# A GEGLU feed-forward kernel: first weight loads reordered over two DMA queues, chunk loads on ScalarE's queue, two of four w_down sums moved

## Chip, cores and metric

One core of a Trainium2 chip. The metric is the device time of one execution in microseconds (us). The kernel before had a median of 542.76 us in the three runs (542.32 to 544.04) from which the prediction was made.

## The reference

```python
B, S, D, F = 1, 2048, 1024, 3584            # bf16, all inputs
def reference(x, w_gate, w_up, w_down):
    return (gelu_tanh(x @ w_gate) * (x @ w_up)) @ w_down
```

## The kernel before

The kernel multiplies with a seven-product scheme (Strassen's). Sums and differences of blocks of x and of the weights are formed on VectorE, GpSimd and ScalarE, and TensorE then does seven block products where a plain product needs eight. It adds them up in banks, accumulators of 128 x 512 values; hT is the hidden activation, stored transposed. Work goes in two halves of 1024 tokens. In a half, 14 pairs of 128-wide column blocks (pairs 0 to 13) give hT, and two groups of down products follow. The first half has plain matmuls in place of pairs 0 and 1, the "first units".

Its first lines issue the loads. `sp` and `act` put an instruction on SyncE's or ScalarE's stream in program order, and a DMA issued there goes to that engine's queue (ScalarE's queue: q10 in the page, 0.79 MB).

```python
load_x0(0, sp)                              # x block, 256 columns
load_w(first, 0, 0, 2, act, 0, FA)          # w_gate rows 0 to 2 (of 8 blocks)
load_w(first, 1, 0, 2, sp, 0, FA)           # w_up rows 0 to 2
load_x0(1, act)
for j in range(2):
    load_xT(xT, 0, 0, KH + j, KH + j + 1)   # DMA transpose, SyncE's queue
    load_w(first, j, 2, 5, act, 0, FA)      # rows 2 to 5, gate then up
act(nc.scalar.preload_act_table(ACT.Gelu_apprx_tanh))
# ... 8 matmuls on constants ...
for j in range(2):
    load_w(first, j, 5, KD, sp, 0, FA)      # rows 5 to 8
for kd in range(KH + 2, KD):
    load_xT(xT, 0, 0, kd, kd + 1)
```

Blocks 0 to 3 of x are transposed on TensorE and copied to xT, blocks 4 to 7 come by DMA transpose. A pair then runs as follows, with hooks (`done`) at which other work is inserted:

```python
# one pair, as it runs from the second on
m1 (2 x 4 bf16 matmuls); ScalarE copies the banks
m2 of the pair before (2 x 4): gelu on ScalarE, hT multiply on VectorE
done("m2 of last")
m6, m6; done("m6"); m5, m5   # m5 overwrites the banks that m2's gelu and multiply read
add m5 to the banks on VectorE; done("m5")
m7, m7; done("m7"); s4 products; done("m3"); a22 products; done("m4")
```

At the hooks of the first half the kernel prepares the down products (`steps`: four w_down sums a pair on VectorE, written to a 4-deep ring of buffers; two of every three are stored to DRAM) and the x of the second half (`stage_x`: DMA transpose into the same ring; `store_x`: store to DRAM):

```python
def load_chunk(key=key):                    # every second pair, 2 x 1 MB
    new_chunk(key)
    for j in range(2):
        load_w(key, j, 0, KD)               # SyncE's queue
...
then["m2 of last"] = [lambda q=q: stage_x(*q) for q in xs[:2]] + then.get("m2 of last", [])
then["m7"] = [store_x]
then["m3"] = steps[:1] + [lambda i=i: stage_load(i) for i in new]
then["m4"] = steps[1:]                      # three sums ahead of the next m2 multiply
```

## Time and profile before

| | kernel before |
|---|---|
| median of the first three runs | 542.76 us |
| span of the profiled execution | 540.9 us |
| TensorE busy | 534.2 us, 99% |
| first pair (pair 2) starts | 34.19 us |
| a pair | 12.56 us; pair 9: 13.16 us |
| x stores, issue to landing | median 5.0 us |

TensorE is the bound (99% busy, 95% of the chain that ended last), so the table is about its stream: when the first pair starts tells what the start cost, and the distance from the first bf16 matmul of one pair to that of the next tells what a pair cost. The lines are in the prediction. A busy sum will not do here: this trace misses 36 matmul records (it has 2356), and busy times of pipelined matmuls overlap (a matmul of L252 has 379 ns in the page's mean, and the next starts 0.216 us after it). In the lines, PE is TensorE and PEld its weight loads, DVE is VectorE, ACT ScalarE, POOL GpSimd; SPq and ACTq are what SyncE and ScalarE issue. A bracket gives how long the engine was idle before, and what ended the wait.

### The profile page before, as it was taken

Reading aid. Unit: us, or ns where it says so; the run is one execution under the profiler, and the core shown is the slowest. Engines: PE = TensorE matmul, PEld = TensorE weight load, DVE = VectorE, ACT = ScalarE, POOL = GpSimd, SP = SyncE. Lnnn points to the kernel's source line nnn. Section 1 sums busy time; section 2 is a strip of 40 time slices with the busy share of each in tenths; the row PEclk is TensorE's granted clock in tenths of the full one; section 3 lists DMA queues with packets and bytes.
Section 4 is the critical chain, followed back from the end, with each engine's and each line's share of the span. In section 5 each row is a group of like instructions: output and inputs, shape, how many; then the busy total and the mean of one; then the engine's idle time right before and its main releaser. Section 6 shows DMA issues by size and latency. Waiting matters only on the chain.

```text
span 540.9 us, 7082 instructions
## 1 busy us (share of the span) xinstructions
PE 534.2 (99%) x2356; PEld 374.8 (69%) x2392; DVE 360.4 (67%) x465; ACT 258.4 (48%) x439; POOL 246.0 (45%) x206
## 2 busy tenths in 40 slices
PE   8999999999999999999999999999999999999997
PEld 3457777766676676767776667777777766866865
DVE  0747878787886998889573433444445469969961
ACT  2435555555555319216465555555554552452270
POOL 0187888888887000000046777667777730000000
PEclk9999999999999999999999999999999999999999
DMA  9926495685837976779950405041331456677846
GB/s 221 307 80 209 125 341 161 211 256 191 277 132 227 333 240 219 266 248 311 331 196 1 155 2 155 4 153 42 114 98 59 155 204 209 228 242 247 288 148 205
DMA packets 84771, 102.70 MB, mean 190 GB/s; under 512 B 18688, under 2 KB 66304, under 8 KB 84736
## 3 DMA queue, kind: packets, MB, share of 16 engines
q1 hardware_dynamic: 83136, 101.47, 58.8%
q10 hardware_dynamic: 1600, 0.79, 0.6%
q8 instruction: 19, 0.31, 0.2%
q14 instruction: 16, 0.13, 0.1%
HBM read 85.98 MB, written 12.58 MB: 182 GB/s over the span
## 4 chain that ended last, share of the span: by engine, by line
PE 95%; DMA 3%; issue 1%; POOL 0%; ACTq 0%; DVE 0%; ACT 0%; SPq 0%
PE bank L388 58%; PE bank L658 32%; PE bank L252 5%; DMA x_dram<-o_sb 2%; DMA w_mem<-in_w_up_dram 1%; POOL s_mem L360 0%; ACTq L161 0%; DVE hT L276 0%; ACT o_sb L711 0%; ACTq L167 0%; SPq L161 0%; DVE o_sb L593 0%; ACTq L711 0%; SPq L612 0%
## 5 line engine op out<-in xcount | busy, mean ns | idle before, releaser
L388 PE MATMUL bank<-t_mem,s_mem 128*128 128x512 f32 x1016 | 240.4, 395 | 0.1
L388 PEld LDWEIGHTS bank<-t_mem,s_mem 128*128 128x128 f32 x1016 | 190.8, 188 | 42.5 <-DVE hT L276 0.5
L360 POOL TENSOR_TENSOR s_mem<-w_mem 128x512 fp32r<-128x512 bf16 x100 | 119.3, 1213 | 191.6 <-DVE t_mem L244 102.2
L658 PE MATMUL bank<-t_mem,s_mem 128*128 128x512 f32 x544 | 127.4, 393 | 0.0
L276 DVE TENSOR_TENSOR hT<-w_mem,bank 128x512 bf16<-128x512 f32 x104 | 70.6, 686 | 75.7 <-PE bank L388 42.5
L658 PEld LDWEIGHTS bank<-t_mem,s_mem 128*128 128x128 f32 x544 | 102.0, 188 | 22.5 <-issue 0.5
L411 DVE TENSOR_TENSOR bank<-bank,m 128x512 f32<-128x512 f32 x104 | 68.0, 694 | 56.2 <-ACT m L433 51.9
L388 PE MATMUL bank<-xT,w_mem 128*128 128x512 bf16 x391 | 93.0, 380 | 1.3
L271 ACT ACTIVATE w_mem<-bank 128x512 f32<-128x512 f32 x104 | 61.0, 596 | 62.3 <-DVE bank L411 39.0
L388 PEld LDWEIGHTS <-w_mem 128*128 128x128 bf16 x416 | 38.7, 98 | 49.8 <-issue 6.3
L360 POOL TENSOR_TENSOR s_mem<-w_mem,s_mem 128x512 fp32r<-128x512 bf16 x50 | 65.8, 1337 | 0.0
L568 DVE TENSOR_TENSOR t_mem<-w_mem 128x1024 fp32r<-128x1024 bf16 x56 | 65.6, 1218 | 0.0
L360 POOL TENSOR_TENSOR s_mem<-s_mem,w_mem 128x512 fp32r<-128x512 f32 x50 | 63.2, 1284 | 0.0
L438 ACT COPY bank<-bank 128x512 f32<-128x512 f32 x52 | 29.6, 570 | 38.2 <-PE bank L388 37.9
L373 ACT CAST s_mem<-w_mem 128x512 fp32r<-128x512 bf16 x52 | 32.0, 615 | 29.1 <-PE bank L388 25.4
L633 DVE TENSOR_TENSOR s_mem<-hT 128x512 fp32r<-128x512 bf16 x52 | 35.7, 714 | 10.2 <-PE bank L658 9.4
L658 PEld LDWEIGHTS <-hT 128*128 128x128 bf16 x224 | 21.3, 98 | 26.6 <-issue 2.1
L433 ACT COPY m<-bank 128x512 f32<-128x512 f32 x52 | 30.5, 587 | 17.4 <-PE bank L388 17.4
L442 ACT COPY bank<-bank 128x512 f32<-128x512 f32 x52 | 29.6, 570 | 13.8 <-PE bank L388 13.8
L711 ACT CAST o_sb<-bank 128x512 bf16<-128x512 f32 x28 | 15.3, 585 | 39.7 <-PE bank L658 39.7
L593 DVE TENSOR_TENSOR o_sb<-wd_sb,o_sb 128x512 fp32r<-128x512 bf16 x28 | 33.6, 1200 | 0.4
L252 PE MATMUL bank<-xT,w_mem 128*128 128x512 bf16 x125 | 28.0, 379 | 0.6 <-DMA w_mem<-in_w_up_dram 0.4
(42 smaller groups left out, 252.4 us busy)
## 6 DMA issues: line engine op xcount, KB each, us to landing
t_mem<-t_dram SPq DMA_DIRECT2D x56, 512.0 KB, 5.3
w_mem<-in_w_gate_dram SPq DMA_DIRECT2D x11, 1024.0 KB, 5.5
w_mem<-in_w_up_dram SPq DMA_DIRECT2D x11, 1024.0 KB, 7.9
wd_sb<-in_w_down_dram SPq DMA_DIRECT2D x28, 256.0 KB, 4.4
t_dram<-o_sb SPq DMA_DIRECT2D x28, 256.0 KB, 2.4
wd_sb<-in_w_down_dram SPq DMA_DIRECT2D x12, 512.0 KB, 8.3
w_mem<-in_w_down_dram SPq DMA_DIRECT2D x10, 512.0 KB, 6.2
w_mem<-in_w_down_dram SPq DMA_DIRECT2D x4, 1024.0 KB, 6.6
```

What stands on the lines that cost most here:

```text
L252: nc.tensor.matmul(ps[:], lhsT=w_sb[:, kd, fi * P : (fi + 1) * P], rhs=xT[tb][:, kd, :], start=(kd == 0), stop=(kd == KD - 1),)
L271: act(nc.scalar.activation(out=g_sb, in_=ps[:], func=ACT.Gelu_apprx_tanh))
L276: nc.vector.tensor_tensor(out=hT[:, fc, tb * TB : (tb + 1) * TB], in0=g_sb, in1=ps[:], op=ALU.mult,)
L360: pool(nc.gpsimd.tensor_tensor(out=t, in0=in0, in1=in1, op=op))
L373: act(nc.scalar.copy(out=t, in_=a(1, 1)))
L388: nc.tensor.matmul(banks[bank][:], lhsT=lhs[:, c, :], rhs=rhs[:, c, :], start=start and c == 0, stop=c == KH - 1, skip_group_check=True,)
L411: nc.vector.tensor_tensor(out=banks[dst][:], in0=banks[src][:], in1=m5[j][:], op=ALU.add)
L433: act(nc.scalar.copy(out=m5[j][:], in_=banks[V_[j]][:]))
L568: dve(nc.vector.tensor_tensor(out=t, in0=in0, in1=in1, op=ALU.subtract))
L593: dve(nc.vector.tensor_tensor(out=t, in0=in0, in1=in1, op=ALU.subtract))
L633: dve(nc.vector.tensor_tensor(out=t, in0=in0, in1=in1, op=op))
L658: nc.tensor.matmul(banks[bset[u]][:], lhsT=lhs(i, u), rhs=rhs(i), start=start and i == 0, stop=stop and i == NS - 1, skip_group_check=True,)
```

## The change

Its intent is to have the weights that TensorE needs first in front of the DMA transposes (the first two took SyncE 1.21 and 1.25 us to issue in the trace of before and landed 5.4 and 5.8 us after issue; the loads around them took 0.45 to 0.74 to issue), and to keep VectorE's w_down sums and the 2 MB chunk loads out of each other's way.

```diff
-    for j in range(2):
-        load_xT(xT, 0, 0, KH + j, KH + j + 1)
-        load_w(first, j, 2, 5, act, 0, FA)
+    load_w(first, 0, 2, 5, act, 0, FA)
+    load_w(first, 1, 2, 5, sp, 0, FA)
@@
-    for j in range(2):
-        load_w(first, j, 5, KD, sp, 0, FA)
-    for kd in range(KH + 2, KD):
+    for kd in range(KH, KD):
         load_xT(xT, 0, 0, kd, kd + 1)
+        if kd == KH + 1:
+            for j in range(2):
+                load_w(first, j, 5, KD, act, 0, FA)
@@ transpose_x0: copies of blocks 0 and 1
-            if n % 2 == 0:
+            if q == 0 or n == 0:
                 dve(nc.vector.tensor_copy(...))
@@ first_units: block by block, gate and up in turn
-        order = [(0, 0), (0, 1), (1, 0), (1, 1)]
-        order += [(j, kd) for kd in range(2, KD) for j in range(2)]
-        for j, kd in order:
+        for kd, j in [(kd, j) for kd in range(KD) for j in range(2)]:
@@ load_chunk
-                        load_w(key, j, 0, KD)
+                        load_w(key, j, 0, KD, act)
@@ hooks of the first half
-                then["m2 of last"] = [
-                    lambda q=q: stage_x(*q) for q in xs[:2]
-                ] + then.get("m2 of last", [])
-                then["m7"] = [store_x]
-                then["m3"] = steps[:1] + [lambda i=i: stage_load(i) for i in new]
-                then["m4"] = steps[1:]
+                then["m2 of last"] = (
+                    then.get("m2 of last", [])
+                    + steps[:2]
+                    + [lambda q=q: stage_x(*q) for q in xs[:2]]
+                )
+                then["m7"] = [store_x] + [lambda i=i: stage_load(i) for i in new]
+                then["m4"] = steps[2:]
@@ the hT differences of pairs 7 to 10 (cut: the w_down rows of pair 12 are appended, not set)
-                then.setdefault("m5", []).append(
+                then.setdefault("m6", []).append(
```

More of the change, by code (lines that the diff above doesn't have):

```diff
@@ L847 @@
                 new = range((n[1] + 2) // 3, (n[2] + 2) // 3)
-                then["m2 of last"] = [
-                    lambda q=q: stage_x(*q) for q in xs[:2]
-                ] + then.get("m2 of last", [])
-                then["m7"] = [store_x]
-                then["m3"] = steps[:1] + [lambda i=i: stage_load(i) for i in new]
-                then["m4"] = steps[1:]
+                then["m2 of last"] = (
[5 more added lines that the diff above has]
+                then["m4"] = steps[2:]
                 xs = xs[2:]
             if pair == NPAIR - 2:
-                then["m2 of last"] = [
-                    lambda: load_wd_rows(0, 4),
-                    lambda: load_wd_rows(4, 8),
-                ]
+                then.setdefault("m2 of last", []).extend(
+                    [lambda: load_wd_rows(0, 4), lambda: load_wd_rows(4, 8)]
+                )
             if 6 < pair < 11:
                 i = 2 * pair - 8
-                then.setdefault("m5", []).append(
+                then.setdefault("m6", []).append(
                     lambda i=i: s_down(hT, 0, "s3", i, i + 2)
```

## The prediction

> **What bounds the kernel now.** I read the page's first and fourth parts, then TensorE's own waits, then TensorE's timeline to see where its stream of matmuls breaks.
>
> ```profile
> PE 534.2 (99%) x2356; PEld 374.8 (69%) x2392; DVE 360.4 (67%) x465; ACT 258.4 (48%) x439; POOL 246.0 (45%) x206
> PE 95%; DMA 3%; issue 1%; POOL 0%; ACTq 0%; DVE 0%; ACT 0%; SPq 0%
> ```
>
> TensorE is busy for 534.2 of 540.9 us and is 95% of the chain that ended last. No other engine is above 67%. Waits elsewhere are therefore worth only what they take out of TensorE's stream. The timeline of TensorE matmuls (start, duration, line, count):
>
> ```profile
> 4.48 0.98 PE L302 MATMUL bank<-ident,w_mem 128*128 128x128 bf16 x8
> 5.54 1.46 PE L252 MATMUL bank<-xT,w_mem 128*128 128x512 bf16 x6
> 6.84 0.61 PE L302 MATMUL bank<-ident,w_mem 128*128 128x128 bf16 x8
> 7.28 1.05 PE L252 MATMUL bank<-xT,w_mem 128*128 128x512 bf16 x4
> 8.71 25.64 PE L252 MATMUL bank<-xT,w_mem 128*128 128x512 bf16 x115 [0.38 <-DMA w_mem<-in_w_up_dram]
> ...
> 107.80 3.63 PE L388 MATMUL bank<-xT,w_mem 128*128 128x512 bf16 x15
> 111.08 9.44 PE L388 MATMUL bank<-t_mem,s_mem 128*128 128x512 f32 x40
> 120.36 3.63 PE L388 MATMUL bank<-xT,w_mem 128*128 128x512 bf16 x15
> 123.64 10.04 PE L388 MATMUL bank<-t_mem,s_mem 128*128 128x512 f32 x40
> 133.52 3.63 PE L388 MATMUL bank<-xT,w_mem 128*128 128x512 bf16 x15
> ```
>
> I use start to start, because busy times of pipelined matmuls overlap. In the chain in order of time, 49 matmuls of the first units take 10.74 us plus a step of 0.05: about 0.216 us each. A pair of the main loop is 56 matmuls in 12.56 us (107.80 to 120.36); less 16 bf16 matmuls at 0.216 (3.46) that leaves 9.10 for 40 fp32r matmuls, 0.228 each. Two breaks show:
>
> - **At the start.** Four matmuls from 7.28 need 0.86 us, so the next could start at 8.14; it starts at 8.71, behind the w_up rows 2 to 5. Loss 0.57 us.
> - **In the pair from 120.36**, pair 9. It takes 13.16 us where its neighbours take 12.56. Loss 0.60 us.
>
> All other pairs of the first half keep 12.56 (within 0.01), as do those of the second. At 40 fp32r and 16 bf16 matmuls a pair the kernel from 8.71 on is otherwise one stream; the down products show two more slips of some 0.13 us. The change can therefore win little more than 1.2 us, 0.2%.
>
> The second break is explained by the VectorE and DMA issue lines around it:
>
> ```profile
> 116.11 0.46 SPq L161 DMA_DIRECT2D w_mem<-in_w_gate_dram  x1
> 116.73 0.46 SPq L161 DMA_DIRECT2D w_mem<-in_w_up_dram  x1
> 117.29 1.99 SPq L612 DMA_DIRECT2D x_dram<-o_sb  x2
> ...
> 125.44 0.69 DVE L593 TENSOR_TENSOR o_sb<-wd_sb 128x512 fp32r<-128x512 bf16 x1 [1.37 <-DMA x_dram<-o_sb]
> 126.05 0.68 DVE L276 TENSOR_TENSOR hT<-w_mem,bank 128x512 bf16<-128x512 f32 x1
> 126.78 1.23 PEld L388 LDWEIGHTS bank<-t_mem,s_mem 128*128 128x128 f32 x6 [0.48 <-DVE hT L276]
> ```
>
> The chunk loads (two of 1 MB) enter SyncE's queue ahead of the two stores of x. A store lands 7.6 us after issue in this stretch (median 5.0 over the kernel). A wd sum on VectorE needs the store's buffer, waits 1.37 us, and holds the hT multiply behind it; that multiply must read its bank before product m5 may overwrite it. In the pair before, three wd sums also stand ahead of that multiply, which then ends at 113.68, about 0.1 us before m5's second half starts: the place has no slack.
>
> [...] ScalarE's queue moved 0.79 MB beside SyncE's from the start, at some 320 GB/s together from 3 to 5 us. [...] one wd sum takes 0.69 us at 99.69, where GpSimd is idle, and two take 3.11 us from 109.98 beside GpSimd sums.
>
> **The change part by part.**
>
> *First weights.* Until now the w_up rows 2 to 5 were the fourth load on ScalarE's queue, issued at 2.38 and landing 6.3 us later (8.68), while SyncE's queue sent slow transposes. After, they are third on SyncE's queue (issue near 1.8). Ahead of any transpose stand 576 KB on each queue: 1.18 MB. Up to 5.0 us the old trace moved 0.84 MB (0.03, 0.17 and 0.64 in the stretches 1 to 2, 2 to 3, 3 to 5); the other 0.34 MB at 320 GB/s takes 1.06. I estimate both weight pieces landed by 6.3 to 6.8.
>
> TensorE then does: transposes from 4.48 and first matmul at 5.54 as before (the copies moved from ScalarE to VectorE end at about the same 5.49); four matmuls of block 0 to 6.40; eight transposes, 0.44, to 6.84; four matmuls of block 1 to 7.70; block 2 at 7.70 without a wait. Before, the same work was reached with ten matmuls done and 8.71. Gain: up to 0.57 us.
>
> What could take it back: rows 5 to 8 are now on ScalarE. The built program makes the w_up piece wait for the w_gate rows 2 to 5[...]. So it is issued near 6.6 to 7.1, where it was 4.96. With only 192 KB ahead of it on its queue and half of the 215 GB/s seen from 5 to 9 us, I estimate a landing at 10.1; it is needed at 7.70 + 14 matmuls of 0.216 = 10.72. The margin is 0.6. The transposes of blocks 4 to 7 are needed at 9.43, 10.29, 11.15 and 12.02 and I estimate them 0.7 to 2 us earlier. The next w_gate half (512 KB) is needed at 12.88; before, it landed 4.7 after issue, at 13.05, and it is now issued about 0.9 earlier: 12.1. All margins are positive but below 1 us, so I credit 0.4 of 0.57.
>
> *Chunk loads on ScalarE.* Ten pairs get two issues of about 0.5 us each on ScalarE. They wait for the m2 matmuls, behind which ScalarE has nothing to do: it is idle 1.24 us before its next copy (112.44). That copy may slip by 0.2 us; its reader, m7, comes almost 2 us later. Cost 0. The x stores lose the 2 MB ahead of them, and no longer take 8 us.
>
> *Two wd sums moved up, x transposes behind them.* The same four sums a pair, but two now stand behind the m2 multiply, not ahead of it, in a stretch where GpSimd is idle (until 114.25). The multiply should end near 112.3 instead of 113.68 against m5's 113.8, so a late store no longer reaches TensorE. The buffers of the x stores are next asked for in the following pair, some 7 us after issue instead of about 4. Gain: the 0.60 of pair 9.
>
> The price: two sums (about 2.0) and, in pairs 7 to 10, an hT difference (0.75) come before the m5 additions. From 112.3 that gives 115.05 and the first addition done at 115.75; TensorE needs its bank at 116.6. Margin 0.85, cost 0.
>
> *Sum:* 0.4 + 0.6 = 1.0 us; 542.76 - 1.0 = 541.7.
>
> **The rivals.**
>
> *The late w_up rows 5 to 8 become the new wait.* For: the semaphore wait ties their issue to a landing. Against: no transposes ahead of them on their queue. A landing at 12 would stall TensorE 1.3 us, and the total would be about 542.4.
>
> *ScalarE is blocked by its DMA issues.* The fourth xT copy stands behind that same issue, so it ends near 8.2 (needed at 8.56); and in the loop a chunk load waiting for an old transfer would hold up every copy. Some tenths in each of ten pairs would be 1 to 3 us more: 543 to 545. Against: the semaphores that the chunk loads wait for belong to transfers issued half a pair or more earlier.
>
> *VectorE's additions come late.* If the moved sums take 1.3 each beside GpSimd, and wait for a load, the first addition misses 116.6 in some of eleven pairs: 0.3 each, about 542.5 to 544. Against: the idle of 1.14 before that addition now.
>
> *All of it is hidden.* Then 542.7. Against: both breaks are gaps in TensorE's own stream, which is the end.
>
> **Range and chances.** All three old runs lie between 542.32 and 544.04, so noise is as big as the effect. I predict 541.7, range 540.9 to 543.0. For 2% faster, 10.9 us would have to go, and TensorE has only 6.7 us of idle in all. For 2% slower a new stall of nearly 1 us in each of ten pairs would be needed.
>
> **What would show it.** Right: TensorE's stream of first-unit matmuls unbroken from about 7.3, the first pair starting near 33.7 (34.19 before); pair 9 lasting 12.56; no wait of a wd sum on an x store; x stores landing in 5 us or less beside chunk loads. Wrong: a TensorE wait near 10.7 on w_up or near 12.9 on w_gate; pairs longer than 12.56, above all the even ones; an m5 addition named as TensorE's releaser.

What the text said of the hardware without a trace or run of this case is cut from it, and the places are marked. The sum: 0.4 for the start and 0.6 for pair 9 make 1.0 us, and 542.76 - 1.0 = 541.7. Of the waits on semaphores the two traces show this much: each of the first eight DMAs to use a semaphore a second time waits on it, and the issue of the w_up rows 5 to 8 is one of these (issued at 7.50, its semaphore's last step at 7.48).

## The result, and the profile after

Ratios here are the mean time of one kernel's fast runs over that of the other's of the same rounds, so not quite the ratio of the medians quoted.

The changed kernel had a median of 541.46 us (541.23 to 543.14, six runs) against 543.1 (542.32 to 544.08, six runs): ratio 0.9973, 95% interval 0.9956 to 0.9991. That is the same within 2%, and clear of 1. It was run twice more: 0.9981 (0.9969 to 0.9993) and 0.9984 (0.9973 to 0.9996). So it is 0.2 to 0.3% faster, about 0.9 to 1.5 us.

The first and fourth parts of its page, for the two lines shown of before:

```profile
PE 535.1 (99%) x2392; PEld 374.5 (69%) x2392; DVE 354.9 (66%) x466; ACT 258.9 (48%) x438; POOL 235.0 (44%) x206
PE 98%; DMA 1%; ACTq 0%; ACT 0%; issue 0%
```

The chain is now 98% TensorE, and DMA is down from 3% to 1%. Busy TensorE time rose from 534.2 to 535.1 because no matmul record is missing here, not because it does more. TensorE's timeline (start, duration, line, count):

```profile
4.38 0.62 PE L302 MATMUL bank<-ident,w_mem 128*128 128x128 bf16 x8 [0.18 <-DMA w_mem<-in_x_dram]
5.24 1.02 PE L252 MATMUL bank<-xT,w_mem 128*128 128x512 bf16 x4 [0.24 <-DVE xT L310]
6.10 0.61 PE L302 MATMUL bank<-ident,w_mem 128*128 128x128 bf16 x8
6.55 27.41 PE L252 MATMUL bank<-xT,w_mem 128*128 128x512 bf16 x124
...
119.98 3.63 PE L386 MATMUL bank<-xT,w_mem 128*128 128x512 bf16 x16
123.25 9.44 PE L386 MATMUL bank<-t_mem,s_mem 128*128 128x512 f32 x40
132.54 3.63 PE L386 MATMUL bank<-xT,w_mem 128*128 128x512 bf16 x16
```

The first pair starts at 33.80 (34.19 before), and pair 9 takes 132.54 - 119.98 = 12.56 (13.16 before). The two account for 0.99 of the 1.2 us between the spans (540.9 and 539.7); two slips of 0.12 and 0.14 in the down products of before, absent here, cover the rest.

The start is less clean than one line of 124 matmuls looks. The timeline of the instructions of several engines:

```profile
7.50 0.44 ACTq L161 DMA_DIRECT2D w_mem<-in_w_up_dram  x1
7.52 0.76 PEld L252 LDWEIGHTS <-w_mem 128*128 128x128 bf16 x5 [0.44 <-DMA w_mem<-in_w_gate_dram]
7.98 0.58 ACT L312 COPY xT<-bank 128x512 bf16<-128x512 bf16 x1 [4.31 <-DMA w_mem<-in_w_gate_dram]
...
10.90 11.12 PEld L252 LDWEIGHTS <-w_mem 128*128 128x128 bf16 x53 [0.47 <-DMA w_mem<-in_w_up_dram]
```

The w_gate rows 2 to 5 land at 7.5. Only then can ScalarE issue the w_up rows 5 to 8, whose semaphore they share, and only behind that issue make its copy of xT block 3. The starts of single matmuls in the trace show three gaps, beyond the spacing of 0.216: 0.11 at 7.53, 0.21 at 8.61 and 0.14 at 10.91, together 0.46 us.

Around pair 9 (SyncE's issues and VectorE, for the lines shown of before):

```profile
113.68 2.83 SPq L605 DMA_TRANSPOSE o_sb<-in_x_dram  x2
121.35 0.80 SPq L610 DMA_DIRECT2D x_dram<-o_sb  x2
...
123.31 0.69 DVE L591 TENSOR_TENSOR o_sb<-wd_sb 128x512 fp32r<-128x512 bf16 x1 [0.96 <-DMA x_dram<-o_sb]
123.92 0.68 DVE L276 TENSOR_TENSOR hT<-w_mem,bank 128x512 bf16<-128x512 f32 x1
```

A sum still waits 0.96 us for a store: this was predicted to vanish. But the multiply ends at 124.60, and m5's second half, which needs it, is due about 126.0 (twelve matmuls of 0.228 after 123.25). That leaves 1.4 us, and TensorE does not notice. The median landing of the eight stores and eight transposes of staged x, from the issue lists of before and then of after, tells what was traded:

```profile
x_dram<-o_sb SPq DMA_DIRECT2D x8, 128.0 KB, 5.0
...
o_sb<-in_x_dram SPq DMA_TRANSPOSE x8, 2.8
```

```profile
x_dram<-o_sb SPq DMA_DIRECT2D x8, 128.0 KB, 2.3
...
o_sb<-in_x_dram SPq DMA_TRANSPOSE x8, 4.7
```

By these medians the stores land 2.7 us sooner after issue, but their transposes land 1.9 us later. In the changed kernel it is the four transposes issued beside chunk loads that take 6.3 to 7.6 us; the other four take 2.7 to 3.2.

### The profile page after: what moved, and what is told of

It is laid out like the page before. It is cut to its first block, busy times and chain, and to the rows that moved or that the text cites. A ratio compares the mean times of both kernels' runs of the same rounds, so it can differ in the third digit from the quotient of the medians.

```text
span 539.7 us, 7102 instructions
## 1 busy us (share of the span) xinstructions
PE 535.1 (99%) x2392; PEld 374.5 (69%) x2392; DVE 354.9 (66%) x466; ACT 258.9 (48%) x438; POOL 235.0 (44%) x206
## 4 chain that ended last, share of the span: by engine, by line
PE 98%; DMA 1%; ACTq 0%; ACT 0%; issue 0%
PE bank L386 61%; PE bank L656 33%; PE bank L252 5%; DMA w_mem<-in_w_gate_dram 1%; ACTq L161 0%; ACT xT L312 0%; ACT o_sb L709 0%; ACTq L167 0%; ACTq L709 0%
## 5 line engine op out<-in xcount | busy, mean ns | idle before, releaser
L358 POOL TENSOR_TENSOR s_mem<-w_mem 128x512 fp32r<-128x512 bf16 x100 | 115.8, 1178 | 201.3 <-DMA w_mem<-in_w_up_dram 104.6
L386 PE MATMUL bank<-xT,w_mem 128*128 128x512 bf16 x416 | 94.3, 380 | 0.0
L358 POOL TENSOR_TENSOR s_mem<-w_mem,s_mem 128x512 fp32r<-128x512 bf16 x50 | 62.1, 1267 | 0.0
L358 POOL TENSOR_TENSOR s_mem<-s_mem,w_mem 128x512 fp32r<-128x512 f32 x50 | 59.6, 1212 | 0.0
L631 DVE TENSOR_TENSOR s_mem<-hT 128x512 fp32r<-128x512 bf16 x52 | 34.2, 685 | 10.2 <-PE bank L656 9.5
L591 DVE TENSOR_TENSOR o_sb<-wd_sb,o_sb 128x512 fp32r<-128x512 bf16 x28 | 29.4, 1051 | 0.5
L252 PE MATMUL bank<-xT,w_mem 128*128 128x512 bf16 x128 | 28.4, 379 | 0.3 <-DVE xT L310 0.2
```

The costliest lines, as they stand in the source:

```text
L252: nc.tensor.matmul(ps[:], lhsT=w_sb[:, kd, fi * P : (fi + 1) * P], rhs=xT[tb][:, kd, :], start=(kd == 0), stop=(kd == KD - 1),)
L358: pool(nc.gpsimd.tensor_tensor(out=t, in0=in0, in1=in1, op=op))
L386: nc.tensor.matmul(banks[bank][:], lhsT=lhs[:, c, :], rhs=rhs[:, c, :], start=start and c == 0, stop=c == KH - 1, skip_group_check=True,)
L631: dve(nc.vector.tensor_tensor(out=t, in0=in0, in1=in1, op=op))
```

## The experiments

Twelve kernels ran, all correct. "First pair" and "pair 9" are read from TensorE's timeline as above. "Down wait" is what a down group (43.95 us, to the next group's or half's start) lost when TensorE waited there for saved sums.

| run | edit | first pair at | pair 9 | down wait | median us | ratio (95%) |
|---|---|---|---|---|---|---|
| before | | 34.19 | 13.16 | no | 542.76 | |
| changed | | 33.80 | 12.56 | no | 541.46 | 0.9973 (0.9956 to 0.9991) |
| e0_after_again | changed | 33.87 | 12.56 | no | 541.45 | 0.9981 (0.9969 to 0.9993) |
| h1_after_third | changed | 34.04 | 13.01 | no | 541.47 | 0.9984 (0.9973 to 0.9996) |
| e1_start_only | start of the change | 33.59 | 13.20 | 1.0 | 542.82 | 0.9997 (0.9983 to 1.0011) |
| e2_loop_only | loop of the change | 33.76 | 12.56 | no | 542.65 | 0.9993 (0.9979 to 1.0008) |
| e3_chunks_act_only | chunk loads to ScalarE | 34.21 | 12.56 | 0.95 | 541.95 | 0.9981 (0.9968 to 0.9994) |
| e4_sums_only | loop, chunks on SyncE | 34.07 | 12.56 | no | 541.77 | 0.9977 (0.9965 to 0.9989) |
| e5_copies_only | one copy to VectorE | 33.55 | 13.25 | 0.66 | 541.97 | 0.9993 (0.9981 to 1.0005) |
| e6_copy_kd3_dve | changed + copy | 33.89 | 12.56 | no | 541.53 | 0.9982 (0.9970 to 0.9994) |
| e7_wup_on_sp | changed + w_up on SyncE | 33.55 | 12.56 | 0.86 | 542.08 | 0.9995 (0.9982 to 1.0007) |
| g1_sums_place | sums' place only | 34.72 | 13.48 | no | 543.88 | 1.0024 (1.0012 to 1.0036) |
| g2_chunks_first | queue order only | 34.54 | 12.56 | 0.76 | 541.86 | 0.9995 (0.9975 to 1.0015) |
| f1_b21_on_act | changed + two loads | 33.87 | 12.56 | no | 542.18 | 0.9995 (0.9983 to 1.0007) |

The ratios are to the kernel before in the same rounds: medians 542.92 for e1 to e4, 542.29 for e0 and e5 to e7, 542.51 for g1, g2, f1, h1.

### The two parts alone

e1 has the diff's hunks up to the first units, e2 those behind them.

> The kernel before with the start of the change alone (order of the first weights, three copies on VectorE, block order). My theory, read from the two traces: the changed kernel's first pair starts at 33.80 us instead of 34.19, and pair 9 takes 12.56 instead of 13.16, and these are separate. So here: first pair starts at 33.8 +- 0.1, pair 9 (from its first bf16 matmul to the next pair's) still 13.0 to 13.2, span some 0.4 us below the kernel before (about 540.5). Rival (the start only pays because the loop part absorbs it, or the other way round): first pair at 33.8 but the end unchanged within 0.1 us, or pair 9 back at 12.56.

> The kernel before with the loop part of the change alone (chunk loads on ScalarE, two sums behind the m2 multiply, x transposes behind them, hT difference after m6). My theory: first pair starts at 34.2 as before, pair 9 takes 12.56, no pair above 12.60; span some 0.6 to 0.85 us below the kernel before. Rival (the loop part gives nothing by itself): pair 9 stays at 13.1 or another pair grows by the same 0.6.

In the traces the parts are separate, as my theory had it: e1 has the early first pair (33.59) and keeps the long pair 9 (13.20); e2 has pair 9 at 12.56. But the first pair of e2, whose start is that of before, came at 33.76 where 34.2 was expected, and the timed runs of neither part alone are clear of noise. e1's own profile loses 1.0 us elsewhere:

```profile
466.71 1.85 PE L656 MATMUL bank<-t_mem,s_mem 128*128 128x512 f32 x7 [0.63 <-DMA t_mem<-t_dram]
```

This is the last block of saved sums, late near the end of a down product. Such a wait stands in 5 of 14 profiles (e1, e3, e5, e7, g2), with old and new code alike, and costs 0.66 to 1.03 us of its group. It is as large as the whole effect. e2's six runs, 541.57 to 543.82, would fit it, but only one of them has a trace, without the wait; so for those runs it is not shown.

### Which edit cures pair 9

e3 is one edit, `load_w(key, j, 0, KD, act)`. e4 is the loop part with the chunk loads left on SyncE.

> The kernel before with one edit: chunk loads on ScalarE's queue, the wd sums where they were. Theory A (the 2 MB ahead of the x stores on SyncE's queue are the cause): x stores land in under 5 us, no wd sum waits over 0.3 us for one, pair 9 takes 12.56. Theory B (the cause is the place of the sums ahead of the m2 multiply; the stores are late with either queue): a wd sum still waits about 1 us for a store, and pair 9 still takes about 13.1. I lean to B, because in the changed kernel an x store was issued at 121.35, 7.7 us after its transpose, and a sum still waited 0.96 us.

> The kernel before with the sums, the x transposes and the hT difference moved as in the change, chunk loads left on SyncE's queue. Theory B (place of the sums): a sum may wait for a buffer, but the m2 multiply ends over 0.5 us ahead of the second half of m5; pair 9 takes 12.56 and the span is 0.6 us below the kernel before. Theory A (2 MB ahead of the stores): pair 9 at 13.0 or more, no gain.

Both have pair 9 at 12.56: e3 came out as theory A had it, against B, and e4 as theory B had it, against A. So the two together single out neither. I had leaned to B. What I had overlooked is that e4 also takes the chunk loads from their place directly ahead of the x stores: in the change's order they go before the x transposes. Two more kernels separate the place of the sums from the order in the queue:

```diff
# g2_chunks_first, from the kernel before: chunk loads ahead of the x transposes, nothing else
-   then["m2 of last"] = [lambda q=q: stage_x(*q) for q in xs[:2]] + then.get("m2 of last", [])
+   then["m2 of last"] = then.get("m2 of last", []) + [lambda q=q: stage_x(*q) for q in xs[:2]]
# g1_sums_place, from the kernel before: sums moved, queue order kept
-   then["m2 of last"] = [lambda q=q: stage_x(*q) for q in xs[:2]] + then.get("m2 of last", [])
-   then["m3"] = steps[:1] + [lambda i=i: stage_load(i) for i in new]
-   then["m4"] = steps[1:]
+   then["m2 of last"] = ([lambda q=q: stage_x(*q) for q in xs[:2]]
+                         + then.get("m2 of last", []) + steps[:2])
+   then["m3"] = [lambda i=i: stage_load(i) for i in new]
+   then["m4"] = steps[2:]
```

> The kernel before with only the place of the wd sums changed: two of the four behind the m2 multiply; the SyncE queue keeps its old order (x transposes, chunk loads, x stores), so the stores still stand behind 2 MB. Theory B (the place of the sums cures pair 9): the multiply of pair 9 ends over 0.5 us ahead of m5's second half and pair 9 takes 12.56. Theory A' (what counts is that nothing of 1 MB stands directly ahead of the x stores on their queue): a sum ahead of the multiply still waits 1 us or more for a store, and some pair from 8 to 10 takes 12.9 or more.

> The kernel before with one edit: on SyncE's queue the chunk loads go ahead of the two x transposes instead of behind them; sums and issuing engine unchanged. Theory A': stores issued later (near 122, the transposes being slower beside the chunks) but landing within 3 us, all sums of pair 9 done in time, pair 9 takes 12.56, about 0.6 us won by the order alone. Theory B: pair 9 stays at 13.0 or more, since three sums still stand ahead of the m2 multiply.

g2 settles which edit is enough: the order in the queue alone gives 12.56 in its trace, though its timed runs (0.9995, 541.07 to 544.74) are not clear of noise. SyncE's issues around pair 9 in g2, and VectorE's wait:

```profile
113.98 0.38 SPq L161 DMA_DIRECT2D w_mem<-in_w_gate_dram  x1
114.53 0.59 SPq L161 DMA_DIRECT2D w_mem<-in_w_up_dram  x1
115.17 4.64 SPq L607 DMA_TRANSPOSE o_sb<-in_x_dram  x2
123.23 0.82 SPq L612 DMA_DIRECT2D x_dram<-o_sb  x2
...
125.17 0.84 DVE L593 TENSOR_TENSOR o_sb<-wd_sb 128x512 fp32r<-128x512 bf16 x1 [0.73 <-DMA x_dram<-o_sb]
125.93 0.67 DVE L276 TENSOR_TENSOR hT<-w_mem,bank 128x512 bf16<-128x512 f32 x1
```

The stores go out six us later than before (117.29 there), yet land 2.1 us after issue instead of 7.6. The waiting sum starts 4.45 us after its pair's start, in the old trace 5.08. That is just enough: the multiply ends at 126.60, and m5's second half is due about 126.7 (its first weight load starts 5.99 after the pair's start, here 120.72, as in undisturbed pairs). e3 has the same 0.1 us to spare (126.28 for 126.38), e4, with the sums moved as well, 1.4 (124.79 for 126.23).

Why the order cures it is not settled by this. In g2 the stores still wait out the 2 MB: the first transpose lands at 123.16, 0.5 us behind the second chunk load (122.68), and only then is its store issued. What every cure has in common is that the chunk loads go out earlier. After the start of pair 8 the first one is issued 8.31 us in the kernel before, 5.82 in g2, 4.49 in e4, 2.86 in e3 and in the changed kernel; the first store then lands 5.06, 4.42, 3.62, 3.55 and 3.25 after the start of pair 9. No run moves the chunk loads away from the stores without also issuing them earlier, so the place in the queue and the time of issue are not separated.

g1 refutes theory B as it stood: moving the sums alone is no cure. Two pairs, 7 and 9, take 13.48. TensorE's timeline in both, and VectorE's in pair 9:

```profile
107.34 2.11 PE L388 MATMUL bank<-t_mem,s_mem 128*128 128x512 f32 x8 [0.53 <-DVE bank L411]
...
133.38 2.11 PE L388 MATMUL bank<-t_mem,s_mem 128*128 128x512 f32 x8 [0.53 <-DVE bank L411]
```

```profile
126.31 0.69 DVE L593 TENSOR_TENSOR o_sb<-wd_sb 128x512 fp32r<-128x512 bf16 x1 [2.74 <-DMA t_dram<-o_sb]
126.92 0.68 DVE L276 TENSOR_TENSOR hT<-w_mem,bank 128x512 bf16<-128x512 f32 x1
...
129.94 1.28 DVE L411 TENSOR_TENSOR bank<-bank,m 128x512 f32<-128x512 f32 x2
131.14 1.57 DVE L633 TENSOR_TENSOR s_mem<-hT 128x512 fp32r<-128x512 bf16 x1
132.64 1.28 DVE L411 TENSOR_TENSOR bank<-bank,m 128x512 f32<-128x512 f32 x2
```

Here too a sum waits for a late store (2.74 us). The line names a store of a sum, which landed at 125.72; but the x store issued at 118.50 landed at 126.23, 0.08 us before the sum began, and its buffer is the one that comes round next in the ring. The multiply is in time (127.60 for 127.84), but the two sums behind it and then the hT difference push the m5 additions past the moment at which TensorE needs their banks. So moving the sums alone turns the wait for the multiply into a wait for the additions, and makes it longer. One caution: g1 leaves the hT difference where it was, and its 1.57 us stand directly ahead of the additions for which TensorE waits. The change moves it as well, so how much of the 0.92 is due to the sums is not shown. The queue order is enough for pair 9, with no slack; the place of the sums adds slack for the multiply on top of it (e4), and takes it from the additions. How much shows in the changed kernel's third run:

> The changed kernel again, as the base for the run before this one and for the spread. Pair 9 at 12.56 in any case. The first pair between 33.55 and 33.9; a wait for saved sums in the down products in fewer than half of such profiles. Median 541.2 to 541.6.

In h1, the changed kernel itself, one store was later than usual, and pair 9 took 13.01. The two x transposes issued between 108 and 124 us landed 8.0 us after issue (median), their stores 2.1. VectorE's timeline and then TensorE's:

```profile
124.56 0.69 DVE L591 TENSOR_TENSOR o_sb<-wd_sb 128x512 fp32r<-128x512 bf16 x1 [1.96 <-DMA x_dram<-o_sb]
...
127.09 1.65 DVE L631 TENSOR_TENSOR s_mem<-hT 128x512 fp32r<-128x512 bf16 x1
128.67 2.48 DVE L409 TENSOR_TENSOR bank<-bank,m 128x512 f32<-128x512 f32 x4
```

```profile
129.50 3.89 PE L386 MATMUL bank<-t_mem,s_mem 128*128 128x512 f32 x16 [0.18 <-DVE bank L409]
```

Its "12.56 in any case" was wrong, and so was its 33.55 to 33.9 for the first pair (34.04).

### What the start is worth

> The changed kernel once more, as the base for the three that follow on this chip. Expected: first matmul of the first units at 5.2 to 5.5, first pair at 33.8 to 34.0, three short stalls between (w_gate rows 2 to 5 near 7.5, the fourth xT copy on ScalarE near 8.5, w_up rows 5 to 8 near 10.9), together about 0.5 us. [...]

The first matmul came at 5.38, not 5.24. e0 has none of the three gaps. Its w_gate rows landed early enough for ScalarE to issue the w_up rows at 6.97, not 7.50. But TensorE was slow for longer: its first eight transposes span 1.03 us, in the changed kernel's first trace 0.62, and its first four matmuls take 1.28 (5.38 to 6.66), there 0.86. That cost it about as much. Two kernels show the two cases of the first transposes and matmuls; e3 has the old start, e1 the new. First e3's timeline of TensorE, then e1's:

```profile
4.59 1.03 PE L302 MATMUL bank<-ident,w_mem 128*128 128x128 bf16 x8 [0.24 <-DMA w_mem<-in_x_dram]
5.65 1.93 PE L252 MATMUL bank<-xT,w_mem 128*128 128x512 bf16 x6
7.42 0.61 PE L302 MATMUL bank<-ident,w_mem 128*128 128x128 bf16 x8
```

```profile
4.62 0.62 PE L302 MATMUL bank<-ident,w_mem 128*128 128x128 bf16 x8 [0.28 <-DMA w_mem<-in_x_dram]
5.48 1.02 PE L252 MATMUL bank<-xT,w_mem 128*128 128x512 bf16 x4 [0.24 <-DVE xT L310]
```

Eight transposes span 1.03 us in e3 and 0.62 in e1. In e3 the six matmuls from 5.65 take 7.42 - 5.65 = 1.77, where six at 0.216 would take 1.30: 0.47 lost. At the transposes the spacing is 0.107 us in some traces and 0.056 in others of the same code (before, e3 and g2 slow, g1 fast), with the eight matmuls on constants ahead in all of them. The granted clock does not show it: it is 1.00 from 4 to 6 us in the trace of before, with transposes 0.107 us apart. Why the rate differs is not shown.

A slow TensorE came to the rows 2 to 5 later and in e2, e3 and e4 did not wait for them: the four matmuls ahead of those rows start there at 7.41, 7.86 and 7.71. In before and g2, slow as well, they start at 7.28 and 7.38, and TensorE then idles 0.38 and 0.49 us; in the fast g1 they start at 7.03, and it idles longest, 0.56 and 0.45.

So one pair of traces cannot price the start. The old start (before, e2, e3, e4, g1, g2) gives first pairs at 34.19, 33.76, 34.21, 34.07, 34.72 and 34.54, mean 34.25. The new (changed, e0, h1, e1, f1) gives 33.80, 33.87, 34.04, 33.59 and 33.87, mean 33.83. The difference is 0.42 us, with a spread of 0.4 to 1.0 within each group. A wait for the rows 2 to 5 of more than 0.3 us is in three of the six old starts (before, g1, g2) and in none of the new.

Two things besides the edit differ between the groups. The slow transposes are not evenly dealt: five of the six old traces have them and two of the five new, and among the slow alone the means are 34.15 and 33.96. And the runs come from several chips. On the two chips that have both starts the new one is earlier each time (chip 6: 33.59 against 33.76 to 34.21; chip 5: 33.87 and 34.04 against 34.54 and 34.72). So the direction is supported; how much of the 0.42 the edit is worth stays open.

> The kernel before with one edit: the second copy of the first block on VectorE, not ScalarE. In the two traces the first matmul on the first weights starts at 5.54 (before) and 5.24 (changed). Theory C (the copy's engine made it earlier): 5.24 here, first pair 0.3 earlier only if the wait for w_up rows 2 to 5 (until 8.71) does not take it back, which it should: 34.2. Theory D ([...] its eight transposes took 0.98 us before and 0.62 after): 5.4 to 5.6 here, and the kernel before and this one differ only in that.

Theory D is that the time of TensorE's eight transposes differs from run to run.

e5 moved one copy and had its first matmul at 5.38, between the two theories' values, and its first pair at 33.55, 0.64 earlier than before. Its w_up rows 2 to 5, issued as in the kernel before, landed at 7.83 and not at 8.66. The gap of 0.57 us on which the prediction was built is therefore one draw of a landing time that lies between 7.83 and 9.20 in the seven traces with that issue order. Traces of one chip lie close (7.89 to 8.03 on chip 6, 9.01 and 9.20 on chip 5), so the chip may be part of it; that was not tested. A trace also shows where time goes: the load's semaphore is raised 16 times, and in the kernel before eleven of these come by 8.10, the other five from 8.36 to 8.66. The transposes vary as theory D has it (eight span 0.84 us here, between the 0.62 and the 1.03 of other traces); what the copy itself does stays open.

> The changed kernel with one more edit: the fourth xT copy on VectorE too, so that it no longer stands behind ScalarE's issue of w_up rows 5 to 8. If that copy costs anything: the stall near 8.5 (0.2 us) goes, but w_up rows 5 to 8, which land at 10.9, then cost more, so the first pair moves by 0.0 to 0.1 only. If the copy is what sets the pace: first pair 0.2 us earlier.

e6 went as the first reading had it: the gap near 8.5 is gone, the wait for w_up at 11.00 is larger (its matmul started 0.32 late), and nothing is won.

> The changed kernel with w_up rows 5 to 8 on SyncE's queue between the second and third transpose, so that they wait for an older load (landed near 4.1) and not for w_gate rows 2 to 5 (7.5). If the shared semaphore is what makes them late: issued near 4.9, landed before 10.4, the fourth xT copy done near 7.6, no stall at 8.5 or 10.9; first pair 0.3 to 0.4 us earlier than in the changed kernel. Rival: the third and fourth transposes, now 0.5 us later, or the next w_gate half, become the new wait and the first pair does not move.

The edit is `load_w(first, 1, 5, KD, sp, 0, FA)` for the w_up piece. From SyncE's queue it is issued at 4.84, not 7.50 as in the changed kernel's trace, because it now shares a semaphore with a load long landed (at 4.11 in the changed kernel's trace). TensorE then has none of the three gaps; one of 0.12 is left at 12.80, where it waits for the next w_gate half (landed at 12.75), which is the rival at a small size. The first pair starts at 33.55, 0.25 ahead of the changed kernel's first trace, a little less than expected. So the shared semaphore was what made it late. As a version it is not shown to win: 0.9995, with a down wait of 0.86 us in its own profile and one run of 543.53.

### The wait for saved sums

```diff
# f1_b21_on_act, from the changed kernel: two of the four lower w_down loads of a down group
-        sp(nc.sync.dma_start(out=w[:, 0 : i1 - i0, :], in_=src))
+        (on ScalarE's queue for q < 2, behind its copies after m5; else as before)
```

> The changed kernel with one more edit: in the down products the first two 0.5 MB loads of the lower left part of w_down are issued by ScalarE behind its copies after m5, not by SyncE directly behind the loads of saved sums. In four of ten profiles so far TensorE waited 0.65 to 1.0 us for the last of the saved sums near the end of m6 (three times) or m4. If those loads crowd it, no such wait here, and the spread of the timed runs is at most 0.6 us, as low as the changed kernel's best; median 541.3. If the late transfer is due to something else, the wait can appear here as well and nothing is gained; if the moved loads come too late, m2 waits for them and it is slower by 1 us or more.

No such wait in the profile, and the closest spread of all (542.00 to 542.31), but 0.7 us slower than h1 in the same rounds. The trace puts that at the very end. Its last copy starts at 536.52, exactly as in e0, but the span is 540.5 and not 539.8: 0.7 us between the last output's copy and the end of the execution. Why is open, and with five of 14 profiles showing the wait elsewhere, one profile without it proves nothing. A first version, with all such loads on ScalarE, deadlocked in the build. No version is shown to beat the changed kernel.

## Why the prediction was right, step by step

- **The size.** Predicted 541.7 within 540.9 to 543.0; measured 541.46. The reasoning "TensorE is the end, so only gaps in its stream count, about 1.2 us" held.
- **Pair 9, 0.60.** Right in size: 13.16 to 13.25 in all three traces with the old loop (before, e1, e5), 12.56 in all with the new (changed, e0, e2, e6, e7, f1, and e4 with the chunk loads on SyncE) except h1's 13.01. Moving the 2 MB out from in front of the stores is the edit that cures (g2, e3); whether by the place in the queue, as named, or by the earlier issue is open. The second cause, that two sums behind the multiply give it slack, is no cure alone: g1 loses 0.92 in each of two pairs. On top of the order it raises the slack from 0.1 to 1.4 us (e4, the changed kernel).
- **"The buffers are asked for some 7 us after issue", no wait of a sum on a store.** Wrong. I took the stores to go out as before, but the transposes ahead of them slow down beside the chunk loads (2.8 to 4.7 us median), so a store went out at 121.35 instead of 117.29. Its buffer was asked for 1.0 us after issue, not 7, and a sum waited 0.96 (e2 1.09, h1 1.96). The "about 4" for the kernel before was a misreading too: 117.29 to 124.07 is 6.8.
- **The start, 0.4 of 0.57.** The sum term came out (0.39 between the two traces, 0.42 between the means), but not by its working, so its fit is partly luck. The 0.57 was not a constant of the old kernel. The w_up rows 2 to 5 landed at 6.4, as estimated; the w_gate rows, estimated for 6.3 to 6.8, came at 7.5 (6.95 to 7.62 in the seven traces with the new order). The bytes went as the estimate had it: by 6.37 ScalarE's queue had moved 0.59 MB, the 576 KB of its first three loads. The failing step was to take a load as landed when its bytes have moved: of the 16 semaphore steps of the w_gate rows, 14 had come by 7.03 and the last at 7.48. Two loads of the same size, issued at 1.78 and 1.82, so took 4.6 us on SyncE's queue and 5.7 on ScalarE's (0.3 to 1.2 us more in the seven traces with this order); why is open. The transposes, estimated 0.7 to 2 us earlier, landed 0.6 and 0.3 us later for blocks 4 and 5 and 1.2 and 1.4 earlier for 6 and 7, without a gap.
- **The rival of late w_up rows 5 to 8.** Partly real: issued at 7.50 (estimated 6.6 to 7.1), landed at 10.9 (10.1), for a gap of 0.14 and not the 1.3 of the rival.
- **The rival of ScalarE held up by its issues.** Real at the start: the fourth xT copy, estimated to end near 8.2, ended at 8.56, and TensorE's matmul came 0.21 late. In the loop it did not show.
- **Chunk loads on ScalarE cost nothing.** Right: no pair of e2 or of the changed kernel's first trace is above 12.56.
- **Margin of 0.85 for the m5 additions.** Right on most traces, where the first addition is done 7.73 us after the pair's start for a matmul due at 8.93; in h1 a late store delayed it to 9.12, and the pair lost 0.45. This rival was real, but seldom.

## What to carry to other kernels

Here a large load (2 MB) stood in a queue directly ahead of a small transfer (128 KB) on whose landing a buffer depended, and changing the order in that queue alone took pair 9 from 13.16 to 12.56 us without touching the engine that waited (g2). In such a place try the order, and look then whether it was the order or the earlier issue that helped. A gap seen in one trace of a DMA-fed start may be one draw (here a landing between 7.83 and 9.20 us in seven traces): before pricing it, look at the same code in several traces, other kernels' included. For effects of 0.2%, the distance between two instructions in the trace resolves what medians with 2 us of spread can't (here 0.60 us of pair 9, in runs of the kernel before from 542.32 to 544.08).
